# A spectral filter and a gated feed-forward block on one core: remainder blocks placed by small DMAs, first weights in pieces, one normalizing operation, the down projection in halves

## The chip, the cores and the metric

The kernel runs on one core of one Trainium2 chip. The metric is the device time of one execution in microseconds (us); lower is better. A core has five engines that each work through a list of instructions in order: TensorE (PE in the profile; its weight loads are a row of their own, PEld), VectorE (DVE), ScalarE (ACT), GpSimd (POOL) and SyncE (SP). SP issues most DMAs, POOL the others. Engines wait for one another on semaphores.

## The reference

The input x is [1, 2048, 576] in bf16. Two residual blocks follow each other:

```
def _A_ref(x, w_r, w_i):                     # spectral filter
    X = rfft2(x.astype(float32), axes=(-2, -1))
    X = X * (w_r + 1j * w_i)                 # w_r, w_i: [2048, 289]
    return irfft2(X, s=(2048, 576), axes=(-2, -1)).astype(bfloat16)

def _B_ref(x, w_gate, w_up, w_down):         # 576 -> 4608 -> 576
    return (gelu(x @ w_gate) * (x @ w_up)) @ w_down

h  = x + _A_ref(layernorm(x), w_r, w_i)
h2 = h + _B_ref(layernorm(h), w_gate, w_up, w_down)
```

The layer norms have no weights; gelu is the tanh form.

## The kernel before

The 2048 rows lie as 16 tiles of 128 rows in XO (tile c, 576 columns). The program is written as one list of operations; a helper, `Prog`, records for each what it reads and writes and puts in the semaphore waits. The order on every engine is the order in which operations are recorded, so a wait at the head of an engine's list holds up everything behind it. Three orders are written out by hand as strings of tokens.

**First stage (`SEQ1`, up to about 20 us).** The first layer norm's statistics, and the first step of the transform over rows, into U. SP loads x, tables and the filter weights (WS) meanwhile.

**Transform stage (`SEQF`, about 20 to 46 us).** For each of 16 groups i the list has: D (a matmul over columns; lower case d is its second half with the evacuation into CUS), B (matmul, evacuation into YS), T (two DVE multiplies of YS with the filter weights WS: the main 256 columns into TP, line 673, and the remaining 32 into TR), V (matmul, v its second half with the evacuation into V, line 607) and, for every four groups, R (matmul of the collected remainders TR). `VENG`, `DENG` and `BENG` say whether ACT or DVE evacuates. R's result goes through ACT into RB (line 703), and `st_R` then places it in VR by DVE multiplies with a mask of ones and zeros, MK (line 711): a block of 32 partitions of VR must hold its own group's numbers and zeros elsewhere. Before `SEQF` starts, POOL copies parts of WS to the other half of the partitions by DMA (`dup_w`). Behind the last of these, SP loads the tables DT and IT and the identity IDT (lines 747 to 749); `wg_load(0, 0)` at line 750 then loads the first quarter of the gate weights (POOL) and of the up weights (SP), each as one transfer of 512 rows and one of 64. `wg_load(1, 1)` and `wg_load(2, 2)` follow after `SEQF`.

**Inverse stage (`SEQ`, about 46 to 58.5 us).** For tiles 0 to 7: I (matmul of V and, in the second half i, of VR with DT, lines 802 to 809), E (its evacuation into GS; A, D and S name the engines: ACT, DVE, split), N and o (matmul with IT), a (add into XO on DVE, line 831). For tiles 0 to 3 also: s (sum of squares), q and c (square root and reciprocal), n (`norm`, lines 854 to 860: two operations, 576 columns and then the last 64 columns once more, so that HN has 640), u and U (transposes on TensorE with IDT), e (evacuation into HT0), and at last G0 and G1, the first gate/up products in two parts of 256 rows.

**Feed-forward part (from about 58.5 us).** Four blocks of 512 rows. In each, `gu_part` (line 917) computes gate and up for 36 column blocks f of 128, as 64-row matmuls of 512 columns that run in pairs on the two halves of the array; ACT applies gelu (line 925) and DVE multiplies (line 926) into AT. In the first block the inverse stage of tiles 8 to 15 is mixed in (`def_i`, `def_n`). Then `down` (lines 997 to 1009) multiplies AT by WD for four tiles of 128 rows: per tile two column halves of 288, each 36 matmuls with all 128 rows of the array (line 1004), then the residual add (line 1007) and the store. The last tile splits 448 and 128. The tiles of the next block are normalized and transposed by DMA while TensorE works.

Of the kernel before, what the change touches and what calls it, by code (L numbers as in the profile page):

```python
# [15 lines left out]
NT = 16  # L16
# [11 lines left out]
SEQF = """D1 D0 d1 D2 d0 d2 B1 D4 B0 d4 D3 T1 B2 T0 d3 D5 V1 d5 T2 v1 D6 B3 d6 B4 V0 B5 T3 v0 D7 T4 D8 d7 B6 d8 V3 R0 T5 v3 T6 r0 V2 B7 v2 D9 V5 d9 D10 v5 d10 V4 B9 T7 D12 v4 d12 B8 D11 T9 B10 d11 R1 D13 T8 T10 r1 d13 D14 B11 V6 d14 V7 v6 v7 T11 B12 V8 D15 v8 B13 T12 d15 B14 T13 V9 v9 T14 R2 r2 B15 V10 V12 v10 V13 v12 R3 T15 r3 V11 v13 V14 v11 v14 V15 R4 v15 r4""".split()  # L28
VENG = [('act',), ('dve',), ('act',), ('act',), ('act', 'dve'), ('act', 'dve'), ('act', 'dve'), ('act', 'dve'), ('act',), ('act',), ('act',), ('act',), ('act',), ('act',), ('act', 'dve'), ('act', 'dve')]
DENG, BENG = ['act', 'act', 'dve', 'act', 'act', 'act', 'dve', 'act', 'dve', 'act', 'act', 'act', 'dve', 'act', 'act', 'dve'], ['act', 'act', 'act', 'act', 'act', 'act', 'act', 'act', 'act', 'act', 'act', 'act', 'act', 'act', 'act', 'act']  # L30
QR = ((0, 1), (1, 2), (2, 3), (3, 4), (4, 8), (8, 16))
DEF0, DSTEP = 3, 4
SEQ = """I3 I1 i3 I2 E3S i1 i2 E1S N3 I0 o3 i0 a3 N1 E2A N2 E0S o1 I7 a1 s3A o2 N0 i7 o0 q3 s1A a2 c3 I5 a0 E7A s2D I6 q1 i5 E5A c1 s0D i6 E6A N7 I4 o7 n3P i4 q2 a7 n1P u3 q0 N5 U3 E4A c0 o5 e3A c2 u1 n2P U1 e1A N6 n0D u0 o6 U0 N4 a5 u2 e0A a6 U2 o4 G0 e2D a4 G1""".split()
# [296 lines left out]
def _build(nc, A_x, A_w_r, A_w_i, B_w_gate, B_w_up, B_w_down, out):  # L330
# [20 lines left out]
    VR = sb.alloc("VR", [128, NT, NG, 2, 4], BF16)  # L351
# [21 lines left out]
    MK = sb.alloc("MK", [128, 2, 8], BF16)  # L373
# [37 lines left out]
    RB = sb.alloc("RB", [128, 2, 2, NT, 2, 4], BF16)  # L411
# [217 lines left out]
    def wg_load(j, slot):  # L629
        f0, f1 = 1152 * j, 1152 * j + 1152  # L630
        tile = wg_tile(slot)
        for o, (eng, src) in enumerate(((POOL, B_w_gate), (SP, B_w_up))):
            P.dma(eng, tile[:, 4 * o:4 * o + 4, :], src[0:512, f0:f1].rearrange("(t p) f -> p t f", p=128), f"wgu{o}{j}{slot}", w=[("WG", slot, o)])
            P.dma(eng, tile[64 * o:64 * o + 64, 8, :], src[512:576, f0:f1], f"wgu{o}{j}{slot}", w=[("WG", slot, 2 + o)])
# [57 lines left out]
    def st_R(q, second):  # L692
        js = [i for i in range(4 * q, 4 * q + 4) if i < LAST] if q < 4 else [LAST]
        g0, n, b0 = GORD[js[0]], len(js), FB["R", q]

        def mm(h, o, t_, first, last, after):
            return P.op(PE, lambda t: t.matmul(bank(b0 + o, 0, 128, 0, 128), TR[64 * h:64 * h + 64, q % 2, o, t_, :], VT[64 * h:64 * h + 64, 1 + o if q == 4 else 0, t_, :], start=first, stop=last),
                        r=[("TR", q % 2, j) for j in range(4)] + ["VT"], w=[("PS", b0 + o)], after=after)

        halves(("R", q), second, [[0, 1]] * 2, mm)  # L700
        if not second:
            return
        ev(ACT, RB[:, q % 2, :, :, :, :].rearrange("p t n o e -> p o (t n) e"), banks(b0, 2, 128).rearrange("p o (a e) -> p o a e", e=4),
           [("PS", b0), ("PS", b0 + 1)], [("RB", q % 2)])
        for u in range((n + 1) // 2):
            m = min(2, n - 2 * u)
            for t_ in range(2):
                dst = VR[64 * t_:64 * t_ + 64, :, g0 + 2 * u:g0 + 2 * u + m, :, :].rearrange("p n g o e -> p n g (o e)")
                src = RB[64 * u:64 * u + 64, q % 2, t_, :, :, :].rearrange("p n o e -> p n (o e)").unsqueeze(2).to_broadcast([64, NT, m, 8])
                msk = MK[64 * u:64 * u + 64, 0:m, :].unsqueeze(1).to_broadcast([64, NT, m, 8])  # L710
                P.op(DVE, lambda v, dst=dst, src=src, msk=msk: v.tensor_tensor(dst, src, msk, op=ALU.mult),  # L711
                     r=[("RB", q % 2), "MK"], w=[("V", GORD[i], 2 + t_) for i in js[2 * u:2 * u + m]])
# [33 lines left out]
    P.op(SP, None, after=[last])  # L746
    P.dma(SP, DT[:, :, :].rearrange("p a b -> p (a b)"), dram["DTAB"][:, :], "dt", w=["DT"])
    P.dma(SP, IT[:, :, :, :].rearrange("p a b c -> p (a b c)"), dram["ITAB"][:, :], "it", w=["IT"])
    P.dma(SP, IDT[:, :], dram["EYE"][:, :], "eye", w=["IDT"])
    wg_load(0, 0)  # L750
    P.dma(SP, DP[:, :, :].rearrange("p a b -> p (a b)"), dram["DPAR"][:, :], "dp", w=["DP"])
    P.dma(SP, ITD[:, :, :].rearrange("p a b -> p (a b)"), dram["IDEF"][:, :], "itd", w=["ITD"])

    for w in SEQF:
        i = int(w[1:].rstrip("abc"))
        if w[0] in "Dd":
            st_D(i, w[0] == "d", DENG[i])
        elif w[0] == "B":
            st_B(i, BENG[i])
        elif w[0] == "T":  # L760
            if w[-1] in "ab":
                st_T(i, (0,) if w[-1] == "a" else (1,))
            else:
                st_T(i)
        elif w[0] in "Vv":
            st_V(i, w[0] == "v", VENG[i])
        elif w[0] in "Rr":
            st_R(i, w[0] == "r")


    P.alias(sum(wkeys, []) + sum(dup, []), [("WG", j, k) for j in (1, 2) for k in range(4)])
    for j in range(1, 3):
        wg_load(j, j)
# [3 lines left out]
    vtail = [("V", g, c) for g in range(NG) for c in range(2, 4)]  # L777
# [24 lines left out]
    def i_mm(c, second):  # L802
        b, e = SLOT["I", c], ends.setdefault(("I", c), [None, None])
        for j in range(2 + second):
            for r in range(2):
                o, r0 = r ^ (not second), 64 * r
                lhs = V[r0:r0 + 64, j, o, c, :, :, :] if j < 2 else VR[r0:r0 + 64, c, :, :, :]
                e[o] = P.op(PE, lambda t, r0=r0, o=o, j=j, lhs=lhs: t.matmul(bank(b + o, 0, 128, 0, KW), lhs, DT[r0:r0 + 64, 2 * o + j if j < 2 else 4, 0:KW], start=(not second and j == 0), stop=(second and j == 2)),  # L808
                            r=vk[j] + ["DT"], w=[("PS", b + o)], after=[e[o]] if second and j == 0 else [])
# [44 lines left out]
    def norm(c, eng=DVE):  # L854
        hs = c % 4
        q = lq(c)
        for i, (o0, o1, x0, x1) in enumerate(((0, D, 0, D), (D, 640, 512, D))):
            P.op(eng, lambda v, c=c, hs=hs, o0=o0, o1=o1, x0=x0, x1=x1: v.tensor_scalar(HN[:, hs, o0:o1], XO[:, c, x0:x1], NM[:, c:c + 1],
                                                                                        RS2[:, c:c + 1], op0=ALU.add, op1=ALU.mult),
                 r=[("X", c), ("NM", c), ("RS2", q)], w=[("HN", hs, i)])  # L860

    def turn_dma(c):
# [3 lines left out]
        for k in range(5):  # L866
            P.dma(SP, HT[:, k, 128 * (c % 4):128 * (c % 4) + 128], HN[:, hs, 128 * k:128 * k + 128], f"tr{c}",
                  r=[("HN", hs, 0), ("HN", hs, 1)], w=[("HT", q % 2, c % 4, k)], transpose=True)

    def turn_mm(c, second):  # L870
        hs, b0, e = c % 4, SLOT["u", c], ends.setdefault(("u", c), [None, None])
        plan = ((3, 0), (4, 1)) if second else ((0, 2), (1, 3), (2, 4))
        for j, ks in enumerate(plan):
            for r, k in enumerate(ks):
# [3 lines left out]
                            r=[("HN", hs, 0), ("HN", hs, 1), "IDT"], w=[("PS", b0 + o)], after=[e[o]] if second and j == 0 else [])  # L878
# [25 lines left out]
    def gu_part(m, second, c0=0, c1=512):  # L904
# [5 lines left out]
        for j in range(n):  # L910
            for half in range(2):
                o, wt = seqs[half][j]
                kt = 4 if wt == 8 else wt % 4
# [36 lines left out]
    fdead = ["DT", "IT", "J0", "J1", "ZD"] + [(n_, c) for n_ in ("ATB", "ATS") for c in range(NT)] + [("G", i // 2, i % 2) for i in range(10)] + [*[("Y", a) for a in range(NY)], ("RB", 0), ("RB", 1)]  # L950
# [4 lines left out]
    def def_i(c, second):  # L955
        e = ends.setdefault(("X", c), [None, None])
        for j in range(3):
            for r in range(2):
                o, r0 = r ^ (not second), 64 * r
                t_ = j if j < 2 else r  # L960
                lhs, rhs = (V[r0:r0 + 64, o, t_, c, :, :, :], DP[r0:r0 + 64, 2 * o + t_, :]) if j < 2 else (VR[r0:r0 + 64, c, :, :, :], DP[r0:r0 + 64, 4 + o, :])
# [35 lines left out]
    def down(tb, p):  # L997
        c = 4 * tb + p

        cut = 448 if c == NT - 1 else 288  # L1000
        for h, (d0, d1) in enumerate(((0, cut), (cut, D))):
            b = 2 * (p % 2) + h
            for k, f in enumerate([*range(36)] if tb == 0 else [*range(9, 36), *range(9)]):
                P.op(PE, lambda t, b=b, d0=d0, d1=d1, f=f, p=p: t.matmul(bank(b, 0, 128, 0, d1 - d0), AT[:, f, 128 * p:128 * p + 128],  # L1004
                                                                        WD[:, f, d0:d1], start=(f == 9 * (tb > 0)), stop=(f == (8 if tb else 35))),
                     r=[("AT", f), ("WD", f // 4)], w=[("PS", b)])
            P.op(DVE, lambda v, b=b, d0=d0, d1=d1, p=p, c=c: v.tensor_tensor(OS[:, p % 2, d0:d1], bank(b, 0, 128, 0, d1 - d0), XO[:, c, d0:d1], op=ALU.add),  # L1007
                 r=[("PS", b), ("X", c)], w=[("OS", p % 2, k) for k in (range(2) if d1 == cut and cut > 288 else (h,))])
            P.dma(SP, ov[:, c, d0:d1], OS[:, p % 2, d0:d1], f"so{p % 2}{h}", r=[("OS", p % 2, h)], w=[("OUT", p % 2, h)])
# [3 lines left out]
    for tb in range(4):  # L1013
# [26 lines left out]
        for p in range(4):  # L1040
            down(tb, p)
# [37 lines left out]
```

## Time and profile before

| what | value |
|---|---|
| median of 3 runs | 490.61 us (489.57 to 491.44) |
| profiled execution | 489.82 us, span 487.8 us |
| granted TensorE clock | 1.000 of full speed |
| PE busy in the span | 479.1 us, 98% |
| DVE / ACT / POOL busy | 188.6 / 147.2 / 43.2 us |
| masked multiplies, DVE (line 711) | 18, 0.22 to 0.29 us each |
| matmuls of down (line 1004), 288 columns | 1080 recorded, 286 ns each |
| norm on DVE (line 858) | 425 ns for 576 columns and 295 ns for 64 |
| norm on POOL (line 858) | 923 ns for 576 columns and 560 ns for 64 |
| output store | 1.6 us from issue to landing |

The span is the time from the first to the last instruction of the profiled execution; its time is 2.0 us longer. Matmuls are pipelined: a matmul's own duration (286 ns) is longer than the distance to the next one's start, so the distance is what counts. In a timeline line the first number is the start, the second the time from the first start to the last end of the xN instructions that were merged. For DMAs the row of the queue (SPq) is the time of issuing, not of moving the data.

### The profile page before, as it was taken

Reading aid. Unit: us, or ns where it says so; the run is one execution under the profiler, and the core shown is the slowest. Engines: PE = TensorE matmul, PEld = TensorE weight load, DVE = VectorE, ACT = ScalarE, POOL = GpSimd, SP = SyncE. Lnnn points to the kernel's source line nnn. Section 1 sums busy time; section 2 is a strip of 40 time slices with the busy share of each in tenths; the row PEclk is TensorE's granted clock in tenths of the full one; section 3 lists DMA queues with packets and bytes.
Section 4 is the critical chain, followed back from the end, with each engine's and each line's share of the span. In section 5 each row is a group of like instructions: output and inputs, shape, how many; then the busy total and the mean of one; then the engine's idle time right before and its main releaser. Section 6 shows DMA issues by size and latency. Waiting matters only on the chain.

```text
span 487.8 us, 10721 instructions
## 1 busy us (share of the span) xinstructions
PE 479.1 (98%) x4791; PEld 286.9 (59%) x4792; DVE 188.6 (39%) x389; ACT 147.2 (30%) x294; POOL 43.2 (9%) x77
## 2 busy tenths in 40 slices
PE   7998999999999999999999999999999999999998
PEld 3876675555577744444577644444677444444775
DVE  7898746666511134333311144333211233333011
ACT  6997754343400022233200022332100123323000
POOL 5852631000300000000000000000000000000000
PEclk9999999999999999999999999999999999999999
DMA  8969998211350000100000001000000000000000
GB/s 283 231 160 321 353 329 270 74 26 26 110 170 20 16 18 19 23 1 1 1 19 19 13 20 23 15 1 2 6 19 19 7 1 1 1 0 1 13 19 18
DMA packets 25533, 32.65 MB, mean 67 GB/s; under 512 B 11664, under 2 KB 18096, under 8 KB 25488
## 3 DMA queue, kind: packets, MB, share of 16 engines
q1 hardware_dynamic: 22048, 18.27, 13.0%
q0 software_dynamic: 3440, 13.70, 8.8%
q8 instruction: 37, 0.61, 0.5%
q14 instruction: 8, 0.07, 0.1%
HBM read 26.01 MB, written 2.36 MB: 58 GB/s over the span
## 4 chain that ended last, share of the span: by engine, by line
PE 91%; DVE 3%; DMA 2%; POOL 2%; ACT 1%; issue 1%; DVEq 0%; POOLq 0%
PE PS L917 57%; PE PS L1004 29%; PE PS L537 1%; DMA WS<-WS 1%; DVE TP L673 1%; DVE XO L831 1%; DMA WS<-in_A_w_r_dram 1%; ACT U L563 1%; PE PS L962 1%; POOL WS L725 1%; POOL WS L240 1%; PE PS L808 0%; DVE VR L711 0%; PE PS L979 0%; PE PS L825 0%
## 5 line engine op out<-in xcount | busy, mean ns | idle before, releaser
L917 PE MATMUL PS<-HT,WG 64*128 64x512 bf16 (+1 forms) x2142 | 233.5, 372 | 0.0
L917 PEld LDWEIGHTS PS<-HT,WG 64*128 64x128 bf16 x2142 | 109.8, 94 | 111.0 <-issue 0.9
L925 ACT ACTIVATE GL<-PS 128x512 bf16<-128x512 f32 x144 | 85.7, 596 | 282.4 <-PE PS L917 274.4
L926 DVE TENSOR_TENSOR AT<-GL,PS 128x512 bf16<-128x512 bf16 x144 | 98.8, 687 | 165.1 <-ACT GL L925 165.1
L1004 PE MATMUL PS<-WD,AT 128*128 128x288 bf16 (+2 forms) x1152 | 141.8, 286 | 0.0
L1004 PEld LDWEIGHTS PS<-WD,AT 128*128 128x128 bf16 x1152 | 111.0, 98 | 31.5 <-ACT GL L925 1.3
L1007 DVE TENSOR_TENSOR OS<-PS,XO 128x288 bf16<-128x288 f32 (+2 forms) x32 | 14.6, 458 | 123.3 <-PE PS L1004 123.3
L917 PE MATMUL PS<-HT,WGX 64*128 64x512 bf16 x486 | 53.4, 376 | 0.0
L917 PEld LDWEIGHTS PS<-HT,WGX 64*128 64x128 bf16 x486 | 23.7, 94 | 28.8
L640 PE MATMUL PS<-FT,U 64*128 64x288 bf16 x160 | 14.1, 284 | 0.3 <-DVE V L607 0.2
L834 ACT ACTIVATE OS<-XO,NM 128x576 bf16<-128x576 bf16 x14 | 10.8, 774 | 11.4 <-DVE XO L983 11.4
L681 PE MATMUL PS<-VT,TP 64*128 64x128 bf16 x256 | 11.2, 217 | 0.1
L673 DVE TENSOR_TENSOR TP<-YS,WS 128x1024 bf16<-128x1024 bf16 x16 | 11.0, 689 | 0.4 <-ACT YS L607 0.2
L240 POOL DMA_DIRECT2D WD<-in_B_w_down_dram x9 | 6.8, 759 | 49.1 <-PE PS L979 49.1
L563 ACT ACTIVATE U<-PS 128x384 bf16<-128x384 f32 (+2 forms) x31 | 10.5, 427 | 1.4 <-PE PS L552 1.3
L495 DVE BATCH_NORM_STATS2 ST<-XO 128x6 f32<-128x288 bf16 x26 | 10.0, 441 | 1.9 <-DMA XO<-in_A_x_dram 1.7
L607 ACT ACTIVATE YS<-PS 128x576 bf16<-128x576 f32 x16 | 10.1, 661 | 0.3 <-PE PS L660 0.2
L552 PE MATMUL PS<-ATS,XO 128*128 128x128 bf16 x96 | 8.1, 219 | 1.9 <-POOL ATS L521 1.7
L681 PEld LDWEIGHTS PS<-VT,TP 64*128 64x128 bf16 x256 | 8.4, 94 | 2.1 <-PE PS L681 0.2
L537 PE MATMUL PS<-ZD 128*128 128x512 bf16 x19 | 7.5, 560 | 1.5 <-POOL ZD L430 1.5
L552 PEld LDWEIGHTS PS<-ATS,XO 128*128 128x128 bf16 x96 | 6.9, 98 | 3.1 <-POOL ATS L521 2.5
L640 PEld LDWEIGHTS PS<-FT,U 64*128 64x128 bf16 x160 | 7.0, 94 | 2.7 <-DVE V L607 0.7
(83 smaller groups left out, 213.5 us busy)
## 6 DMA issues: line engine op xcount, KB each, us to landing
WD<-in_B_w_down_dram POOLq DMA_DIRECT2D x9, 576.0 KB, 13.1
WG<-in_B_w_gate_dram POOLq DMA_DIRECT2D x4, 1152.0 KB, 9.8
WG<-in_B_w_up_dram SPq DMA_DIRECT2D x4, 1152.0 KB, 9.4
out_dram<-OS SPq DMA_DIRECT2D x30, 72.0 KB, 1.6
XO<-in_A_x_dram SPq DMA_DIRECT2D x3, 576.0 KB, 7.2
WGX<-in_B_w_up_dram SPq DMA_DIRECT2D x1, 1152.0 KB, 5.6
WGX<-in_B_w_gate_dram POOLq DMA_DIRECT2D x1, 1152.0 KB, 9.9
HT<-HN SPq DMA_TRANSPOSE x60, 2.4
```

The lines of the kernel that those rows point to most:

```text
L240: fn = lambda e: e.dma_start(out_ap, in_ap)
L537: P.op(PE, lambda t: t.matmul(bank(b), ZD[:, 0:128], ZD[:, :], start=True, stop=True), r=["ZD"], w=[("PS", b)])
L552: P.op(PE, lambda t, b=b, lhs=lhs, p0=p0, p1=p1, s=s, e=e, o=o, c=c: t.matmul(bank(b, p0, p1, o, o + 128), lhs, ATS[:, c, :], start=s, sto ...
L563: fn = (lambda v: v.tensor_copy(dst, src)) if eng == DVE else (lambda a: a.activation(dst, src, ACTF.Copy))
L640: return P.op(PE, lambda t: t.matmul(bank(b0 + o, 0, 128, 0, 2 * HK), U[64 * h:64 * h + 64, us, 2 * i:2 * i + 2, :, :], FT[64 * h:64 * h + ...
L673: P.op(DVE, lambda v, dst=dst, y4=y4, w4=w4: v.tensor_tensor(dst, y4, w4, op=ALU.mult), r=[("Y", sl), *dup[(i >= 5) + (i >= 8) + (i >= 12) ...
L681: return P.op(PE, lambda t: t.matmul(bank(b0 + o, 0, 128, 128 * c, 128 * c + 128), TP[64 * h:64 * h + 64, z, o, t_, c:256:2], VT[64 * h:64 ...
L917: op = P.op(PE, lambda t, h0=h0, kt=kt, wt=wt, b=b, s=(not second and j == 0), e=(second and j == n - 1): t.matmul(bank(b, 0, 128, c0, c1) ...
L925: P.op(ACT, lambda a: a.activation(GL[:, s2, :], bank(b0), ACTF.Gelu_apprx_tanh), r=[("PS", b0)], w=[("GL", s2)])
L926: P.op(DVE, lambda v: v.tensor_tensor(AT[:, f, :], GL[:, s2, :], bank(b0 + 1), op=ALU.mult), r=[("GL", s2), ("PS", b0 + 1)], w=[("AT", f)])
L1004: P.op(PE, lambda t, b=b, d0=d0, d1=d1, f=f, p=p: t.matmul(bank(b, 0, 128, 0, d1 - d0), AT[:, f, 128 * p:128 * p + 128], WD[:, f, d0:d1], ...
L1007: P.op(DVE, lambda v, b=b, d0=d0, d1=d1, p=p, c=c: v.tensor_tensor(OS[:, p % 2, d0:d1], bank(b, 0, 128, 0, d1 - d0), XO[:, c, d0:d1], op=A ...
```

## The change

Four edits, with the hand-written orders and engine choices redone around them:

1. **Remainder blocks.** VR gets another layout ([128, 16 groups, 2, 4, 16 tiles] instead of tiles first) and is set to zero by POOL at the start; MK and the masked multiplies are gone. For R0 to R2, RB is evacuated as before (R0 by DVE, R1 and R2 by ACT) and eight DMAs per R on SP, of 32 partitions with 256 bytes each, put the blocks where they belong. For R3 and R4 ACT and DVE evacuate straight from PSUM into VR, a block of 32 partitions at a time. The permutation moves into R's matmul, whose right operand is read with a step.
2. **First weights.** The first quarter of gate and up is loaded by SP in ten pieces; each piece waits until TensorE has done everything recorded before a token of the order (`LOADS`). The tables DT, IT and IDT are issued behind r1, DP and ITD behind i6. Slots 1 and 2 and WD are issued after the first gate/up product, G0.
3. **One normalizing operation.** The 640 columns of HN are written by one operation that reads XO as two overlapping runs of 320 columns; the weight tiles' order follows that.
4. **Down in halves.** All tiles but the last use 64-row matmuls in pairs, in two passes per tile; the halves change places in the second pass, and the passes of different tiles are interleaved ("0 1 0 2 1 3 2 3").

```
+SEQF = """D1 D0 d1 D2 d0 d2 B1 D3 B0 T1 T0 d3 D4 B2 d4 D5 V1 T2 d5 v1 D7 B4 d7 B3 D6 B5 d6 V2 T4 V0 T3 v2 v0 D8 B7 T5 d8 D10 B6 d10 D9 T6 B8 d9 D11 R0 T7 d11 V5 r0 V3 v5 v3 V4 B9 v4 D13 B10 d13 T8 V6 D12 v6 T9 d12 V7 T10 V9 v7 R1 v9 r1 B11 B13 T11 D14 B12 T12 d14 D15 V8 d15 v8 B14 T13 T14 R2 r2 B15 V10 V11 v10 V13 v11 V12 v13 T15 v12 V14 V15 v14 v15 R3 R4 r3 r4""".split()
+VENG = [('act', 'dve'), ('dve',), ('act', 'dve'), ('act',), ('act',), ('act', 'dve'), ('act',), ('act', 'dve'), ('dve',), ('act', 'dve'), ('act',), ('act',), ('act', 'dve'), ('act',), ('act', 'dve'), ('act', 'dve')]
+DENG, BENG = [... 'dve' at 2 and 7, else 'act'], [... 'dve' at 6, 9 and 11, else 'act']
+LOADS = {"r1": "t", "v8": "0", "v10": "1", "v11": "2", "v13": "3", "v12": "4", ".i0": "5", ".i1": "6", ".N3": "7", ".i4": "8 9", ".i6": "d"}
+RENG = ['dve', 'act', 'act', 'act', 'act']
+SEQ = """I2 I3 i2 E2A I0 i3 i0 N2 I1 o2 E3A i1 E0S a2 N0 N3 o0 I4 o3 E1S s2A q2 a0 N1 i4 s0A E4A a3 o1 c2 q0 I6 I5 n2P a1 i6 i5 s3D E6A I7 c0 N4 E5A i7 s1D n0P o4 a4 u2 N6 U2 E7A o6 q1 q3 c1 u0 N5 U0 c3 o5 n3P e2A n1D e0A u1 U1 N7 e1A a6 u3 a5 o7 a7 U3 e3D G0 G1""".split()
...
-    P.op(POOL, lambda g: g.memset(MK[:, :, :], 0.0), w=["MK"])
...
+    P.op(POOL, lambda g: g.memset(VR[:, :, :, :, :], 0.0), ...)
...
     # st_R
-        ev(ACT, RB[:, q % 2, ...], banks(b0, 2, 128)..., [("RB", q % 2)])
-        ... P.op(DVE, lambda v, dst=dst, src=src, msk=msk: v.tensor_tensor(dst, src, msk, op=ALU.mult), ...)
+        if q < 3:
+            ev(RENG[q], RB[:, q, :, :, :, :].rearrange("p t o e n -> p o t (e n)"), banks(b0, 2, 128).rearrange("p o (t x) -> p o t x", t=2), keys, [("RB", q)])
+            for j, i in enumerate(js):
+                for t_ in range(2):
+                    P.dma(SP, VR[64 * t_ + 32 * (j % 2):64 * t_ + 32 * (j % 2) + 32, GORD[i], :, :, :], RB[32 * j:32 * j + 32, q, t_, :, :, :], f"r{q}", ...)
+            return
+        for j, i in enumerate(js):
+            for e, o0, o1 in (((ACT, DVE)[j], 0, 2),) if q == 3 and j < 2 else ((ACT, 0, 1), (DVE, 1, 2)):
+                for t_ in range(2):
+                    ... ev(e, dst, src, keys[o0:o1], [("V", GORD[i], 2 + t_, o0)])
...
+    def hold(eng=SP):
+        P.op(eng, None, after=[P.ops[PE][-1]])
+    def tab_load():
+        P.op(SP, None, after=[last])
+        ... DT, IT, IDT
+    def tab2_load():
+        hold()
+        ... DP, ITD
+    def wg0_part(k):
+        hold()
+        src = (B_w_gate, B_w_up)[k % 2]
+        if k < 8:
+            P.dma(SP, WG3[:, 0, 4 * (k % 2) + k // 2, :], src[(0, 128, 320, 448)[k // 2]:(128, 256, 448, 576)[k // 2], 0:1152], "wg00")
+        else:
+            P.dma(SP, WG3[64 * (k % 2):64 * (k % 2) + 64, 0, 8, :], src[256:320, 0:1152], "wg00", ...)
...
     # norm
+        x2 = bass.AP(x.tensor, x.offset, [list(x.ap[0]), [256, 2], [1, 320]])
+        P.op(eng, lambda v: v.tensor_scalar(HN[:, hs, :].rearrange("p (a b) -> p a b", a=2), x2, NM[:, c:c + 1], RS2[:, c:c + 1], op0=ALU.add, op1=ALU.mult), ...)
...
     for w in SEQ:
         ...
+        loads("." + w)
+        if w == "G0":
+            hold(SP), hold(POOL)
+    for j in range(1, 3):
+        wg_load(j, j)
...
+    def down_pass(tb, p, second):
+        fs, b0 = forder(tb), 2 * ((3, 0, 1, 2)[p] if tb == 0 else p)
+        e = ends.setdefault(("Z", tb, p), [None, None])
+        for j, f in enumerate(fs):
+            for r in range(2):
+                h, r0 = r ^ second, 64 * r
+                e[h] = P.op(PE, ... matmul(bank(b0 + h, 0, 128, 0, 288), AT[r0:r0 + 64, f, 128 * p:128 * p + 128], WD[r0:r0 + 64, f, 288 * h:288 * h + 288], ...)
+        if second:
+            for h in range(2):
+                down_out(tb, p, h, 288 * h, 288 * h + 288, b0 + h, False)
...
+        for w in "0 1 0 2 1 3 2 3".split() if tb < 3 else "0 1 0 2 1 2".split():
+            first = ("Z", tb, int(w)) not in ends
+            down_pass(tb, int(w), not first)
+    down_last(3, 3)
```

More of the change, by code (lines that the diff above doesn't have):

```diff
@@ L912, in gu_part @@
                 o, wt = seqs[half][j]
-                kt = 4 if wt == 8 else wt % 4
+                kt = 2 if wt == 8 else (0, 1, 3, 4)[wt % 4]
                 h0 = 64 * half
@@ L995, in deferred, with down_out @@
             fn(c, second)
-    def down(tb, p):
+    def down_out(tb, p, h, d0, d1, b, both):
         c = 4 * tb + p
-        cut = 448 if c == NT - 1 else 288
+        P.op(DVE, lambda v: v.tensor_tensor(OS[:, p % 2, d0:d1], bank(b, 0, 128, 0, d1 - d0), XO[:, c, d0:d1], op=ALU.add),
+             r=[("PS", b), ("X", c)], w=[("OS", p % 2, k) for k in (range(2) if both else (h,))])
+        P.dma(SP, ov[:, c, d0:d1], OS[:, p % 2, d0:d1], f"so{p % 2}{h}", r=[("OS", p % 2, h)], w=[("OUT", p % 2, h)])
@@ new lines, in forder @@
+    def forder(tb):
+        return [*range(36)] if tb == 0 else [*range(9, 36), *range(9)]
+    def down_pass(tb, p, second):
[4 more added lines that the diff above has]
+                h, r0 = r ^ second, 64 * r
+                e[h] = P.op(PE, lambda t, f=f, h=h, r0=r0, j=j: t.matmul(bank(b0 + h, 0, 128, 0, 288), AT[r0:r0 + 64, f, 128 * p:128 * p + 128], WD[r0:r0 + 64, f, 288 * h:288 * h + 288],
+                                                                         start=(not second and j == 0), stop=(second and j == 35)),
+                            r=[("AT", f), ("WD", f // 4)], w=[("PS", b0 + h)], after=[e[h]] if second and j == 0 else [])
+        if second:
+            for h in range(2):
+                down_out(tb, p, h, 288 * h, 288 * h + 288, b0 + h, False)
@@ L1001, in down, with down_last @@
+    def down_last(tb, p):
+        cut = 448
         for h, (d0, d1) in enumerate(((0, cut), (cut, D))):
[L1002 to L1005, printed above, removed]
+            b = 2 * p + h
+            for j, f in enumerate(forder(tb)):
+                P.op(PE, lambda t, b=b, d0=d0, d1=d1, f=f, j=j: t.matmul(bank(b, 0, 128, 0, d1 - d0), AT[:, f, 128 * p:128 * p + 128], WD[:, f, d0:d1], start=(j == 0), stop=(j == 35)),
@@ L1006, in down @@
                      r=[("AT", f), ("WD", f // 4)], w=[("PS", b)])
-            P.op(DVE, lambda v, b=b, d0=d0, d1=d1, p=p, c=c: v.tensor_tensor(OS[:, p % 2, d0:d1], bank(b, 0, 128, 0, d1 - d0), XO[:, c, d0:d1], op=ALU.add),
-                 r=[("PS", b), ("X", c)], w=[("OS", p % 2, k) for k in (range(2) if d1 == cut and cut > 288 else (h,))])
-            P.dma(SP, ov[:, c, d0:d1], OS[:, p % 2, d0:d1], f"so{p % 2}{h}", r=[("OS", p % 2, h)], w=[("OUT", p % 2, h)])
+            down_out(tb, p, h, d0, d1, b, h == 0)
```

76 lines of the change are left out of this document (33 added, 43 removed).

## The prediction

> **What bounds the kernel now.** I read the page first, then the chain of waits, then busy time by stage, then the timelines of the queues that the change touches.
>
> ```profile
> span 487.8 us, 10721 instructions
> PE 479.1 (98%) x4791; PEld 286.9 (59%) x4792; DVE 188.6 (39%) x389; ACT 147.2 (30%) x294; POOL 43.2 (9%) x77
> ```
>
> ```profile
> 28.93 5.47 DMA WS<-WS
> ...
> 45.36 0.75 DVE V L607 x2
> 46.10 0.14 issue
> 46.24 1.89 PE PS L808 x28
> 48.13 0.54 issue
> ...
> 58.61 6.25 PE PS L917 x92
> ...
> 133.79 35.39 PE PS L1004 x288
> 169.17 70.04 PE PS L917 x648
> ```
>
> From 58.6 us on, the chain is TensorE alone: gate/up (L917) and down (L1004), four times over, to 485.5. No wait there is worth removing; only the cost of a matmul and of the switch between the two forms counts. Whatever else the change can win lies ahead of 58.6.
>
> ```profile
> 20.98:34.44 13.46, 13.45 (x268) 10.09 (x264) 12.68 (x29) 12.85 (x26) 9.52 (x18) 1.00 0.66 161
> 34.44:46.57 12.13, 10.75 (x254) 8.14 (x250) 11.85 (x35) 10.68 (x24) 1.92 (x3) 1.00 1.01 318
> 46.57:58.55 11.98, 10.49 (x183) 6.95 (x179) 8.91 (x22) 8.90 (x20) 6.18 (x10) 1.00 1.03 340
> ```
>
> The columns after the window are its length, then busy PE, weight loads, DVE, ACT, POOL. In the middle stage DVE is busy 11.85 of 12.13 us: it bounds it. The stage starts at 34.4, when the second copy of WS has landed (first fence). In the last stage before the feed-forward part no engine is full.
>
> **The change part by part.** All terms are against the profiled execution (span 487.8, its time 489.82; the median of the three runs shown is 490.61, 0.79 above it).
>
> *Down in halves.* Each 128-row matmul of 288 columns becomes two of 64 rows on the two halves of the array. Cadence: 288 of the old in 35.39 us is 0.1229 each; ten 64-row ones of the same width (23.66, last fence) are five pairs: (0.78 - 0.284) / 4 = 0.124, within reading error. So one pair costs what one matmul did: 15 tiles x 72 pairs stay as they were, and each ns by which I am wrong costs 1.08 us. What goes is the switch of form:
>
> ```profile
> 132.96 0.83 PE L917 MATMUL PS<-HT,WG 64*128 64x512 bf16 x6
> 133.72 0.42 PE L1004 MATMUL PS<-WD,AT 128*128 128x288 bf16 x2
> ```
>
> ```profile
> 168.52 0.65 PE L1004 MATMUL PS<-WD,AT 128*128 128x288 bf16 x4
> 169.11 0.39 PE L917 MATMUL PS<-HT,WG 64*128 64x512 bf16 x2
> ```
>
> The last gate/up matmul starts at 132.96 + 0.83 - 0.376 = 133.41, down 0.31 later instead of 0.216; the way back is 169.11 - (168.52 + 0.65 - 0.286) = 0.22 instead of 0.123. That is 0.095 each. There are seven; the last tile keeps the old form, so one comes back: 6 x 0.095 = 0.6 us won. The semaphore that a tile's second pass waits for belongs to a pass with another tile's 4.4 us pass behind it: no cost.
>
> *Masked multiplies go.* DVE loses 18 of them: 14 x 0.29 + 4 x 0.22 = 4.9 us. It gains evacuations moved by the new order (three YS at 0.67, V shares, one RB, six small tail pieces at about 0.2) and loses three CUS. From T8 on I count 8 x 0.74 (T), 0.67 (B11), 0.66 (v8), 5 x 0.35 (V halves), 6 x 0.2 (tail): 10.2 us from 34.44, so 44.7, with some stalls 45.2, against 46.57 before. T8 would be ready by 33.5, but waits for the copy that lands at 34.40, because what releases it upstream is untouched. ACT comes out equal (27.5 against 27.8 us summed).
>
> *The small DMAs.* R0, R1 and R2 issue eight each on SP, 24 in all, and SP takes its list in order: R0, R1, then DT, IT and the identity (placed behind r1 now, at 37.50 before), weight piece 0, then R2. Behind R2 wait pieces 1 to 9 and the second tables. The waits for TensorE themselves hold nothing up before R2: v8's matmuls are done near 40, SP gets there after 42. The first I matmul that reads VR waits for R2's last landing. So the spacing s of SP's issues is the crux. Rows:
>
> ```profile
> 2.60 0.43 SPq L240 DMA_DIRECT2D ATB<-c_atab  x1
> 3.07 0.91 SPq L240 DMA_DIRECT2D XO<-in_A_x_dram  x2
> ...
> 23.06 1.23 SPq L240 DMA_DIRECT2D WS<-in_A_w_r_dram  x2
> ```
>
> Plain two-dimensional loads at the start follow each other at 0.47; strided 32-row ones at 23 us at 0.64; a lone one takes 0.33 (DT, the output stores), so 0.37 with the gap. The new ones are plain, with few rows: I take 0.47 and keep 0.37 and 0.64 as ends. R1's evacuation by ACT stands behind V9, which waits for T9: 34.44 + 1.48, matmuls and evacuation, some 37.0. From there: 8 x 0.47 = 40.8; three tables 1.5, 42.3; piece 0, 42.8; R2, 46.55; landing as the stores do, 1.6: 48.15. This is later than DVE's 45.2 and decides. Before, the same point (VR read, 46.98 in the timeline) stood at about 47.0. At 0.37 it is 46.2; at 0.64 R0 itself runs to 38.0 and the point is 52.6. (R0 starts near 32.9: from 22.1, where the copies of WS end, DVE has 8.6 us of work ahead of T7 in the new list, 0.8 of stalls, T7 and the RB evacuation.) For any spacing that the trace shows, SP ends after DVE: the multiplies' 4.9 us are not what is won.
>
> R's right operand is now read with a step of 4 elements, VR's weights with 16. TP's weights with a step of 2 load in 94 ns like contiguous ones, so I take nothing; if such a load took twice that, 24 pairs would be 0.07 us longer, 1.6 us.
>
> *From there to the first gate/up.* Before, POOL's norms made it late:
>
> ```profile
> 52.45 1.69 POOL L858 TENSOR_SCALAR HN<-XO,NM,RS 128x576 bf16<-128x576 bf16 x2 [5.15 <-DVE RS L844]
> 54.31 1.75 POOL L858 TENSOR_SCALAR HN<-XO,NM,RS 128x576 bf16<-128x576 bf16 x2 [0.17 <-POOL HN L858]
> 56.23 1.32 POOL L858 TENSOR_SCALAR HN<-XO,NM,RS 128x576 bf16<-128x576 bf16 x2 [0.17 <-DVE HN L858]
> ```
>
> Three pairs, 5.1 us, then 1.0 to the first gate/up at 58.55. One operation of 640 columns costs 0.92 x 640/576 = 1.03, so the row shrinks to 3.3, and DVE's own chain takes over: a2 starts 2.2 after the VR point (rest of I2, its evacuation, N2 and o2), then 5.8 us of DVE work to the last reciprocal, 1.15 for POOL's last norm, 0.55 for u3, o7, U3: 9.7, with stalls 10.2 (9.7 to 11.3). Before, 46.98 to 58.55 took 11.6. So gate/up starts at 48.15 + 10.2 = 58.35, 0.2 earlier. DVE's norms inside the feed-forward part get shorter under TensorE's cover: nothing.
>
> *Weight pieces.* Before, the gate half was issued at 31.83 and shared the DMA engines with the tables (DT took 5.1 us to land). Now pieces 8 and 9 leave when i4 is done, 4.3 after the VR point; two issues and a landing of some 3 us end at about 8.3, under 10.2. Cover is 1.9 us. Slots 1 and 2 and WD start at 58 instead of 44; slot 1 is read 20 us later and took 15 at most. POOL's fill of VR: from ZD's 0.53 for 512 columns, 2048 cost 1.8, ending at 3.45 against the first x at 3.70, hidden.
>
> **Sum.** -0.6 (switches) - 0.2 (start of gate/up) = -0.8: 489.0 for the profiled execution; on the footing of the median 489.8.
>
> **The rivals.**
>
> *SP is quick* (0.25). At 0.37 the VR point is 46.2 and gate/up starts at 56.4: -2.2 - 0.6 = -2.8, 487.8; with the shorter 9.7, or with DVE's 45.2 as the limit, down to 486.3. For it: the lone issues at 0.33. Against: no train in the trace is so dense.
>
> *SP is slow* (0.20), the one that ends slower. At 0.64 the VR point is 52.6 and gate/up starts at 62.8: +4.25 - 0.6 = +3.7, 494.3. For it: SP's W loads keep that spacing, whatever their size. Against: they are strided, and issued while x and W fill the DMA engines. It decides over the bound from s = 0.60 on (point at 51.3, +2.4).
>
> *Issue rate of TensorE* (0.04). Down now starts a matmul and a weight load every 61 ns, for 35 us at a stretch. If pairs settled at 124 ns instead of 122.6, it would cost 1080 x 1.4 = 1.5 us: 491.3. Against: the V stage starts 64-row matmuls of 128 columns in pairs 56 to 60 ns apart.
>
> ```profile
> 41.69 0.82 PE L681 MATMUL PS<-VT,TP 64*128 64x128 bf16 x22
> ...
> 23.66 0.78 PE L640 MATMUL PS<-FT,U 64*128 64x288 bf16 x10
> ```
>
> The Trainium skill (TensorE: Matmul & The Clock Gate, "Wait — 56ns, not 53.3ns?") says that without hardware decode about 62 ns go into each matmul, a bound once the array's work is shorter; a pair would be 124 ns. Here 22 matmuls start within 0.82 - 0.217 us, 29 ns each, so the trace does not bear that bound out.
>
> *The change does not reach the path* (0.03): the last weight piece lands later than 10.2 after the VR point, as late loads did here (10.6 us for the gate rest). It would then add what it is late, 1 to 4 us, 491 to 493.5.
>
> **How the numbers follow.** The forecast has 0.48. A measurement of this kernel can tell about 0.5%, 2.45 us, from no change. The quick case is faster by more than that in most of its chance, and the forecast's own short side adds a little: faster 0.27. Slow SP beyond 0.60 and late weights: slower 0.19. The rest, 0.54, lies within. The range takes the quick case at 9.7 on its low side and the slow one up to s = 0.62 on its high side: 486.6 to 493.6. The forecast's own range, s from 0.42 to 0.56, is 488.7 to 491.9.
>
> **What would show it.** Right: SP's small DMAs 0.45 to 0.5 apart; TensorE waiting at its first VR matmul near 48 while DVE and ACT idle; gate/up first at about 58.3; 36 pairs of down in 4.41 us; no gap over 0.13 at the switch; norms on POOL near 1.03. Wrong: the VR matmul released by DVE or ACT (SP quick), or after 51 (SP slow); pairs over 123 ns; a first gate/up that waits for WG.

## The result and the profile after

The changed kernel takes 496.49 us (median of 4 runs, 495.86 to 497.51), the kernel before 490.86 beside it (4 runs, 489.57 to 491.44): ratio 1.012, 95% interval 1.0092 to 1.0148. It is slower, and 2.9 us above the upper end of the range predicted. The profiled execution took 496.92 us. From its page:

```profile
span 495.1 us, 12880 instructions
...
PE 479.8 (97%) x5872; PEld 282.4 (57%) x5872; DVE 182.9 (37%) x367; ACT 147.6 (30%) x296; POOL 44.9 (9%) x72
...
PEclk9999699999999999999999999999999999999999
```

TensorE's busy time is nearly what it was (479.8 for 479.1); the span grew by 7.3 us. One slice of 12.4 us, the fifth, was not granted the full clock. The chain of waits shows what stands there:

```profile
42.18 1.59 SPq L243
...
51.48 1.76 DMA VR<-RB
53.38 2.38 PE PS L829 x18
...
62.63 1.43 POOL HN L880
66.52 6.20 PE PS L938 x92
```

Where the chain before ran from DVE's last evacuations straight into the I matmuls at 46.24, it now goes through SP's queue, through a landing in VR, and reaches gate/up (L938) at 66.5 instead of 58.6. Busy time by stage (length; busy PE, weight loads, DVE, ACT, POOL; granted clock; DMA share; GB/s):

```profile
34.44:46.57 12.13, 9.85 (x244) 7.90 (x238) 10.88 (x29) 10.71 (x26) 0.00 (x0) 1.00 0.12 22
46.57:53.38 6.81, 1.05 (x13) 0.46 (x14) 0.00 (x0) 0.00 (x0) 0.00 (x0) 0.67 0.53 180
53.38:59.15 5.77, 5.77 (x49) 4.16 (x51) 1.60 (x3) 2.88 (x6) 0.00 (x0) 0.50 0.83 260
59.15:66.42 7.27, 6.91 (x127) 4.89 (x124) 6.60 (x15) 6.11 (x14) 3.34 (x3) 1.00 0.62 187
```

DVE did lose the multiplies (it is busy 10.88 us for 11.85, as it took over evacuations) and is done before 46. Then for 6.8 us no engine but TensorE has anything to do, and TensorE itself works for only 1.05 of them; for the next 5.8 us it works at clock 0.50. What the idle stretch waits for is in the timelines of SP's queue and of TensorE:

```profile
32.72 12.32 SPq L243 DMA_DIRECT2D VR<-RB  x16
45.08 0.58 SPq L243 DMA_DIRECT2D DT<-c_dtab  x1
45.70 0.43 SPq L243 DMA_DIRECT2D IT<-c_itab  x1
46.17 0.43 SPq L243 DMA_DIRECT2D IDT<-c_eye  x1
46.65 0.43 SPq L243 DMA_DIRECT2D WG<-in_B_w_gate_dram  x1
47.12 4.95 SPq L243 DMA_DIRECT2D VR<-RB  x8
```

```profile
48.27 1.04 PE L829 MATMUL PS<-DT,V 64*128 64x288 bf16 x12 [3.60 <-DMA DT<-c_dtab]
53.38 0.46 PE L829 MATMUL PS<-DT,VR 64*128 64x288 bf16 x2 [4.07 <-DMA VR<-RB]
```

The sixteen small DMAs of R0 and R1 occupy SP without a pause from 32.72 to 45.04. DT stands behind them and lands at 48.2: TensorE waits 3.6 us. R2's eight end at 52.07 and the last lands at 53.24: it waits 4.1 us more. The clock was halved from 48.91 to 59.15.

The tail went as forecast. The switch of form (last gate/up matmul at 140.25 + 1.46 - 0.376 = 141.33, down at 141.54) is 0.21 instead of 0.31:

```profile
140.25 1.46 PE L938 MATMUL PS<-HT,WG 64*128 64x512 bf16 x12
141.54 1.14 PE L1038 MATMUL PS<-WD,AT 64*128 64x288 bf16 x16
```

Four points are used below for every run, all from the matmuls of the profiled execution: the VR point (first matmul that reads VR), G0 (first gate/up matmul), X (from one to the other) and the tail (from G0 to the last matmul). All are taken from start to start.

| kernel | VR point | X | G0 | tail | clock at one half |
|---|---|---|---|---|---|
| before | 46.98 | 11.57 | 58.55 | 426.68 | none |
| after | 53.38 | 13.04 | 66.42 | 426.09 | 48.91 to 59.15 |

### The profile page after: what moved, and what is told of

It reads as the page before. It is cut to its first block, busy times and chain, and to the rows that moved or that the text cites. A ratio compares the mean times of both kernels' runs of the same rounds, so it can differ in the third digit from the quotient of the medians.

```text
span 495.1 us, 12880 instructions
## 1 busy us (share of the span) xinstructions
PE 479.8 (97%) x5872; PEld 282.4 (57%) x5872; DVE 182.9 (37%) x367; ACT 147.6 (30%) x296; POOL 44.9 (9%) x72
## 4 chain that ended last, share of the span: by engine, by line
PE 88%; DMA 3%; SPq 3%; POOL 2%; DVE 2%; issue 1%; ACT 0%; POOLq 0%; DVEq 0%
PE PS L938 57%; PE PS L1038 27%; SPq L243 3%; PE PS L1050 2%; DMA XO<-in_A_x_dram 1%; DMA WS<-WS 1%; PE PS L846 1%; PE PS L829 1%; DVE ST L495 1%; DMA WS<-in_A_w_r_dram 1%; PE PS L988 1%; POOL WS L729 1%; POOL WS L243 1%; DVE XO L852 0%; PE PS L1005 0%
## 5 line engine op out<-in xcount | busy, mean ns | idle before, releaser
L938 PE MATMUL PS<-HT,WG 64*128 64x512 bf16 (+1 forms) x2142 | 233.3, 372 | 0.0
L938 PEld LDWEIGHTS PS<-HT,WG 64*128 64x128 bf16 x2142 | 106.0, 94 | 114.1 <-DVE AT L947 0.2
L1038 PE MATMUL PS<-WD,AT 64*128 64x288 bf16 x2160 | 132.9, 283 | 0.0
L1038 PEld LDWEIGHTS PS<-WD,AT 64*128 64x128 bf16 x2160 | 103.3, 94 | 29.8
L1025 DVE TENSOR_TENSOR OS<-PS,XO 128x288 bf16<-128x288 f32 (+2 forms) x32 | 13.3, 453 | 125.5 <-PE PS L1038 118.0
L938 PE MATMUL PS<-HT,WGX 64*128 64x512 bf16 x486 | 53.4, 376 | 0.0
L938 PEld LDWEIGHTS PS<-HT,WGX 64*128 64x128 bf16 x486 | 23.2, 94 | 29.2
L829 PE MATMUL PS<-DT,V 64*128 64x288 bf16 x64 | 7.4, 338 | 3.6 <-DMA DT<-c_dtab 3.6
L682 PE MATMUL PS<-VT,TP 64*128 64x128 bf16 x256 | 9.6, 217 | 0.3 <-DVE TP L674 0.3
L243 POOL DMA_DIRECT2D WG<-in_B_w_gate_dram x9 | 6.1, 678 | 34.2 <-DMA WG<-in_B_w_gate_dram 30.6
L1050 PE MATMUL PS<-WD,AT 128*128 128x448 bf16 (+1 forms) x72 | 9.0, 286 | 0.0
L607 ACT ACTIVATE CUS<-PS 128x576 bf16<-128x576 f32 x14 | 8.9, 654 | 0.2 <-PE PS L641 0.2
```

The costliest lines, as they stand in the source:

```text
L243: fn = lambda e: e.dma_start(out_ap, in_ap)
L938: op = P.op(PE, lambda t, h0=h0, kt=kt, wt=wt, b=b, s=(not second and j == 0), e=(second and j == n - 1): t.matmul(bank(b, 0, 128, c0, c1) ...
L1025: P.op(DVE, lambda v: v.tensor_tensor(OS[:, p % 2, d0:d1], bank(b, 0, 128, 0, d1 - d0), XO[:, c, d0:d1], op=ALU.add), r=[("PS", b), ("X", ...
L1038: e[h] = P.op(PE, lambda t, f=f, h=h, r0=r0, j=j: t.matmul(bank(b0 + h, 0, 128, 0, 288), AT[r0:r0 + 64, f, 128 * p:128 * p + 128], WD[r0:r ...
L1050: P.op(PE, lambda t, b=b, d0=d0, d1=d1, f=f, j=j: t.matmul(bank(b, 0, 128, 0, d1 - d0), AT[:, f, 128 * p:128 * p + 128], WD[:, f, d0:d1], ...
```

## The experiments

Theory: SP's train of small DMAs, with the table queued in it, makes TensorE wait, and the wait costs the clock. Rivals: the new order of the transform stage, the normalizing operation, the halves, or the late weights. Medians stand beside the kernel before on the same chip (490.3 to 491.0).

**Half of the small DMAs on GpSimd.**

```
-P.dma(SP, VR[64 * t_ + ...], RB[...], f"r{q}", ...)
+P.dma((SP, POOL)[t_], VR[64 * t_ + ...], RB[...], f"r{q}{t_}", ...)
```

> The changed kernel with half of the small DMAs (one of each pair) issued by POOL, which has nothing to do from 31.8 to 61 us, and the other half by SP; all else as changed. Theory A (SP's train of issues at 0.63 us sets the first VR matmul, at 53.4): R1's four on SP run from 37.9 to 40.4, the tables and piece 0 to 42.4, R2's four to 44.9, the last lands near 46.8. First VR matmul at 46.5 to 48, full clock throughout, first gate/up at 57 to 58.5, time 487 to 490. Theory B (the new orders themselves make the inverse stage longer, about 13 us from the VR matmul to gate/up): VR matmul at 47 too, but gate/up only at 60, time 490.5 or more.

Measured: 492.24 us, ratio 1.0036 (1.0021 to 1.0051). VR point 49.40, G0 62.43, tail 426.08. SP has twelve issues fewer, R1's part of its train ends at 40.8 instead of 45.0, and everything behind it comes 4 us earlier; nearly three quarters of the loss are gone. But X is still 13.04: TensorE stood idle for 1.13 and 2.17 us, and the clock was halved from 48.35 to 55.17. The forecast for the VR point (46.5 to 48) was missed: R2's last DMA is issued at 45.41 and lands at 49.16.

**Dummy matmuls in the wait.** Matmuls of zeros (15 before I2, 18 before its second half) keep TensorE busy.

```
+    def warm(n, b):
+        for _ in range(n):
+            P.op(PE, lambda t: t.matmul(bank(b), ZD[:, 0:128], ZD[:, :], start=True, stop=True), ...)
...
+        if w in ("I2", "i2"):
+            warm(*((15, ...) if w == "I2" else (18, 7)))
```

> The changed kernel with 15 and 18 matmuls on zeros of 128 x 512 put ahead of I2 and i2, so that TensorE does not stand idle while it waits for DT and for VR. The DMAs are untouched, so the first VR matmul stays at 53.4. Theory A1 (the half clock from 48.8 to 59.1 us is a second loss on top of SP's train): full clock, gate/up 1.5 to 2.8 us earlier than 66.4, time 493.7 to 495. Theory B (half clock costs nothing since DVE and ACT set the pace, the order is what is slow): 496 to 497.

```profile
46.87 3.18 PE L960 MATMUL PS<-ZD 128*128 128x512 bf16 x14 [0.16 <-issue]
50.31 0.66 PE L829 MATMUL PS<-DT,V 64*128 64x288 bf16 x8 [0.26 <-DMA DT<-c_dtab]
50.91 4.06 PE L960 MATMUL PS<-ZD 128*128 128x512 bf16 x18
```

Measured: 495.92 us, ratio 1.011 (1.0083 to 1.0137), so the time hardly moved. The trace says why: X fell to 10.29, as it should at full clock, but the VR point stood at 56.09, because in this execution an earlier stretch at half clock (13.2 to 16.6) had moved the whole front back by about 2.4 us (SP's train starts at 35.17 for 32.72). The run shows the price of the half clock behind the wait (13.04 - 10.29 = 2.75 us). The one execution of the four that had the full clock throughout took 494.45, within the 493.7 to 495 expected; by the median the remedy stays inconclusive.

**The masked multiplies back, all else as changed.** VR's layout, MK and the multiplies come from the kernel before, the orders stay new.

> The changed kernel with the first edit alone taken back: VR in its old layout, mask and 18 DVE multiplies, no small DMAs; the new orders, weight pieces, norm and halves stay. Theory A: without the train SP issues the tables at 38 or so, the first VR matmul comes at 46.5 to 48 (DVE is the limit again), gate/up at 57 to 58.5, time 487 to 490. Theory B (orders or weight pieces at fault): gate/up after 59, time 491 or more.

Measured: 490.30 us, ratio 0.9999 (0.9979 to 1.0019). VR point 49.18, X 10.23, tail 426.04, full clock. Undoing the first part alone takes the loss away. It gives no gain: what X and the tail win, the VR point loses. TensorE idles 1.21 us at 39.04 and 1.15 us at 44.67, and its first VR matmul waits for DVE's last multiply. That the new order was not made for these multiplies is the likely reason; the next run bears it out.

**The multiplies back, and the old order of the transform stage.** As the last, with `SEQF` and the engine choices of before.

> The changed kernel with its first part undone (remainder blocks placed by masked multiplies on VectorE) and with the order and the engines of the first stage's work taken from the kernel before; pieces of the first weights, new second order, one normalizing operation and halves stay. Theory (all that is lost lies in part one with its order; the rest is worth about 1.3 us ahead of gate/up and 0.6 behind): first remainder matmul at 46.5 to 47.5 us, 10.3 us to the first gate/up matmul at 57 to 57.8, 426.05 from there on, median 488.3 to 489.3, faster than before by 0.3 to 0.5%. Rival (pieces released by TensorE's progress hold the table or the weights up where the old order runs): first gate/up matmul at 58.5 or later, median 490 or more.

Measured: 488.16 us, ratio 0.9955 (0.9939 to 0.997). VR point 47.50, X 10.24, G0 57.73, tail 426.04. So the other three parts with the new `SEQ` are worth 1.3 us in X and 0.6 in the tail, and the whole loss lies in the first part.

**Parts three and four on the kernel before.**

> The kernel before with the third and the fourth edit alone (one normalizing operation, down in halves). The step of the prediction on halves says 0.6 us less from the first gate/up to the end; the step on norms says that POOL's three norms shrink from 5.1 to 3.3 us and gate/up starts 0.8 to 1.5 earlier than 58.55: time 488.5 to 489.5. Rival (POOL's norms were hidden): gate/up stays at 58.5, time about 490.2.

Measured: 498.89 us, ratio 1.0168 (1.0136 to 1.0199), a miss: VR point 46.78, but X 19.66.

```profile
59.77 1.25 POOL L240 DMA_DIRECT2D WG<-in_B_w_gate_dram  x2 [8.11 <-DMA WG<-in_B_w_gate_dram]
61.07 0.87 POOL L860 TENSOR_SCALAR HN<-XO,NM,RS 128x640 bf16<-128x640 bf16 x1
```

The operation itself is quick (0.87 us). What makes it late is the line above it. The new load of a weight block is two transfers under one key, so the second waits until the first has landed, and GpSimd's list stands still for 8.1 us with the norms behind it. In the changed kernel these loads come after G0, where nothing waits for GpSimd. With keys of their own:

```
-                P.dma(eng, ..., w=[("WG", slot, o)])
+                P.dma(eng, ..., w=[("WG", slot, o + 4 * u)])
```

The operations that read the weights wait for the new keys too.

> The kernel before with one normalizing operation and the down projection in halves, and with the two halves of each 512-row weight load under keys of their own, so that the second does not wait for the first. Theory (these two parts cost nothing by themselves, and the late GpSimd in the run without own keys was that wait): first remainder matmul at 46.8 us, first gate/up matmul at 57 to 58.3, 426.0 us from there to the last matmul, median 488.5 to 490. Rival (one operation of 576 elements as 2 x 320 is itself slow on GpSimd, or halves of loads crowd the queue): first gate/up matmul after 60 us, median over 492.

Measured: 489.26 us, ratio 0.9978 (0.9966 to 0.999). VR point 46.92, X 10.98, tail 426.40 (a late WD transfer holds TensorE's weight loads for 0.49 us at 137). GpSimd's lines L860 start at 52.33, 53.99 and 55.58 and take 0.87, 1.42 and 1.06.

**Down in halves alone on the kernel before.**

> The kernel before with the down projection in halves and nothing else. Theory (a pair of 64-row matmuls costs what one 128-row matmul did, and only the switches of form go): 426.0 to 426.1 us from the first gate/up matmul to the last matmul in place of 426.68, the first gate/up matmul at 58.5 as before, ratio 0.998 to 0.9995. Rival (the pairs settle at 124 ns because TensorE has to start a matmul and a weight load every 61 ns): 427.5 to 427.7 us, ratio 1.001 to 1.003.

Measured: 490.24 us, ratio 0.9991 (0.9977 to 1.0005). The total can't tell 0.6 us from nothing, but the trace can: tail 426.03 against 426.68.

**Tables early, all DMAs on SP.** The table's wait for the last duplicated weight is taken out, and it is issued before the first operation of the transform stage.

```
-LOADS = {"r1": "t", "v8": "0", ...}
+LOADS = {"v8": "0", ...}
     def tab_load():
-        P.op(SP, None, after=[last])
...
+    tab_load()
     for w in SEQF:
```

> The changed kernel with one edit: the three tables of the first stage are issued before the encoder, without the wait for the last duplicated weight; all 24 small DMAs stay on SP. Theory (train and table are two separate losses, and the train alone still sets the first remainder matmul): first table matmul at 44.5 to 45.5 us, the third group of small DMAs is issued from 45.5 on at 0.63 us each and lands at 52, first remainder matmul at 51.5 to 52.5, a wait of 3 to 4.5 us ahead of it, so that the half clock comes again and 12 to 13 us lie between it and the first gate/up matmul; median 494 to 496. Rival (the late table was the cause): first remainder matmul at 47 to 49, full clock, median 488 to 490.

```profile
45.72 0.43 PE L829 MATMUL PS<-DT,V 64*128 64x288 bf16 x4
47.28 0.67 PE L829 MATMUL PS<-DT,V 64*128 64x288 bf16 x8 [1.13 <-DVE VR L607]
51.70 0.46 PE L829 MATMUL PS<-DT,VR 64*128 64x288 bf16 x2 [3.76 <-DMA VR<-RB]
```

Measured: 494.82 us, ratio 1.0097 (1.0061 to 1.0132). The wait for DT is gone, the wait for VR is not. The train alone still sets the VR point, 1.7 us earlier without the tables in it. Half clock 51.19 to 54.61, X 11.63.

**Tables early and half of the small DMAs on GpSimd.** Weight piece 0 also moves behind R2, by `LOADS`.

> The changed kernel with every second small DMA issued by GpSimd, and the three tables of the first stage issued before the encoder starts, without the wait for the last duplicated weight; the first piece of the first weights after r2. Theory (the loss is SP's train of DMAs, the table queued in it, and the half clock that the idle TensorE brings): first table matmul right behind the last tail matmul at about 44.7 us, first remainder matmul at 46.5 to 48.5, no stretch at clock 0.5, 10.3 us from there to the first gate/up matmul, which starts at 56.8 to 58.8; median 488 to 490. Rival (what is left after the DMAs were shared out is the new order, not the table): first remainder matmul at 49.4 as with shared DMAs alone, with a wait of over 3 us ahead of it and half clock behind it; median 492.

```profile
34.73 11.69 SPq L243 DMA_DIRECT2D VR<-RB  x12
46.46 0.58 SPq L243 DMA_DIRECT2D WG<-in_B_w_gate_dram  x1
```

Measured: 488.07 us, ratio 0.9951 (0.9934 to 0.9969). SP's line now has pauses between groups. VR point 48.53, X 10.34 at full clock, G0 58.87, though this execution had lost time to a stretch at half clock at 14.1 to 17.5. The remainder blocks by DMA cost nothing any more once they are off a single queue. That they pay by themselves is not shown: this version and the one with masks in the old order both beat both kernels, by about the same (488.07 and 488.16). By the executions with the full clock throughout they are 487.09 to 487.32 (three of six) and 487.28 to 488.44 (five of six).

**What sets the issue time?** The same 24 DMAs in three other forms. None of them places the remainder blocks; the times alone count.

```
wide_form:   VR[:, g, t_] <- RB[:, q, t_, 0]             128 partitions x 128 bytes, from SBUF
dram_narrow: VR[32 rows, g] <- EYE[32 rows, :]           32 partitions x 256 bytes, from DRAM
dram_wide:   VR[:, g, t_] <- EYE[:, 64 t_:64 t_ + 64]    128 partitions x 128 bytes, from DRAM
```

> The changed kernel, but each of the 24 small DMAs moves 128 partitions x 128 bytes in place of 32 partitions x 256 bytes (twice the bytes, to and from other addresses, so the remainder blocks are not placed and the output's values mean nothing; everything waits as before). Theory A (the issue on SP costs by the form: few partitions are slow): they go 0.47 us apart, the table of the first stage is issued about 41 instead of 45.1 us, TensorE's first remainder matmul starts at 48.5 to 50 us instead of 53.4, the median is 492 to 494. Theory B (0.63 us is what SP needs at that time whatever the form): 0.6 us or more apart, first remainder matmul at 53 to 54 us, median 496 to 497.

> The changed kernel with the 24 small DMAs reading the same 32 partitions x 256 bytes from a constant table in DRAM in place of the evacuated buffer in SBUF (so the remainder blocks are not placed and the output's values mean nothing; waits and destinations as before). Theory C (a source in SBUF makes the issue slow): 0.43 busy, 0.47 apart. Theory D (anything but whole rows of 128 partitions is slow): 0.59 busy, 0.63 apart, first remainder matmul at about 53.4 us.

> As the run before, but 128 partitions x 128 bytes from the table in DRAM (again not the remainder blocks; output without meaning). Theory C (source in SBUF): 0.43 busy, 0.47 apart, first remainder matmul at 49 to 50.5 us. Theory E (128 bytes a partition, or a queue that is already full, is slow whatever the source): 0.60 busy, 0.64 apart, first remainder matmul at 53 to 54. If this one is fast and the 32-partition one slow, both the source's place and the number of partitions count.

The lines of SP's queue for the last group of eight, first `wide_form`:

```profile
47.17 4.97 SPq L243 DMA_DIRECT2D VR<-RB  x8
```

then `dram_narrow`:

```profile
45.10 3.68 SPq L243 DMA_DIRECT2D VR<-c_eye  x8
```

and `dram_wide`:

```profile
45.20 3.75 SPq L243 DMA_DIRECT2D VR<-c_eye  x8
```

A single one takes 0.60, 0.42 and 0.43 us, 0.04 more to the next; the times are 496.18 (median of four runs, ratio 1.0113, 1.0091 to 1.0135), 493.68 and 492.74 (one run each). For these copies, which all end in SBUF, the issue is slow with the source in SBUF, whether 32 or 128 partitions, and quick from the table in DRAM in both forms. Theory A falls; B's numbers came in `wide_form` (VR point 53.50), but the DRAM forms are quick at the same place in the list, so B falls too; C holds for these copies, D and E fall. A source in SBUF alone does not make an issue slow: the output stores, from SBUF to DRAM, take 0.33 us, and 0.43 right behind another. Why the copies inside SBUF are slow is not shown; the strided WS loads from DRAM at 0.64 say that they are not the only slow ones.

The two DRAM forms are also the prediction's own case, issues 0.47 apart. Their VR points are 50.96 and 50.47 instead of 48.15, and both have half clock behind them. So the spacing alone does not account for the miss.

## Why the prediction was wrong, point by point

**The time of SP's train, the step that failed.** The term that was mis-sized is the spacing s, 0.47 for a measured 0.63, and the odd long issue had no term at all. The VR point was to be 48.15 and stood at 53.38, 5.2 us later:

- *0.47 for s.* It was taken from plain loads out of DRAM; between 0.63 and 0.64 was true. R0 and R1 end SP's train at 45.04; the forecast had 40.8. Sixteen issues at 0.63 from 32.72 end at 42.9, so 2.1 us come from the spacing; R2's eight took 4.95 for the 3.75 that they took at 0.47 from DRAM, 1.2 more.
- *Two issues of 1.72 and 1.59 us* (at 35.35 and 42.18, the second in the chain above) make up the other 2.1 us. The sum had no term for them. The kernel before has such ones: its SP timeline at 38.96 shows two weight issues in 2.15 us, one of them of 1.58. `dram_narrow` has two as well, 1.69 in the train and 1.15 at a table.
- The landing took 1.3 us from the end of the last issue instead of 1.6: -0.3. (The stores' 1.6 counts from the start of an issue.)
- R1's evacuation ended at 37.85, not at 37.0. In the changed kernel this is hidden, as SP reaches R1's DMAs at 39.02. In `dram_wide`, where R0's train is shorter, it ended at 38.67, and SP waited for it: part of the 2.3 us by which that VR point came later than 48.15.

The rival "SP is slow" (0.20) named this mechanism, its place and its point of decision: 52.6 against 53.38. That the two are so close is partly luck: it also took the tables at 0.64, which went at 0.47, and had no term for the long issues; its 494.3 lacks the half clock. It got too low a chance because of two arguments. One was that the 0.64 of the WS loads came from DMA engines that were full. They were at 0.12 in this stage, and the spacing stayed. The other was that only strided transfers are slow. A nearer row stood in the trace of before, GpSimd's copies from WS to WS, the only plain copies there inside SBUF: six in 3.59 us, 0.60 each. It is a hint and no more, for GpSimd's loads of WS from DRAM took 0.58 and 0.60 as well.

```profile
28.27 3.59 POOL L240 DMA_DIRECT2D WS<-WS  x6 [2.10 <-issue]
```

**A missing term: the clock.** X was to be 10.2 and measured 13.04. At full clock it is 10.2 to 10.3: 10.23 (`masked`), 10.24 (`masked_oldorder`), 10.29 (`warm_clock`), 10.34 (`tables_first`), 10.27 in the middle. So the working of X was right, and the 2.8 us are the half clock, which no rival had:

| kernel | TensorE idle before the VR point, us | half clock behind the VR point | X above 10.27 |
|---|---|---|---|
| after | 3.60 and 4.07 | 5.77 us | 2.77 |
| split_issue | 1.13 and 2.17 | 5.77 | 2.77 |
| dram_narrow | 2.38 and 2.55 | 4.16 | 1.97 |
| dram_wide | 0.67, 0.29 and 2.94 | 3.22 | 1.51 |
| wide_form | 3.77 and 3.40 | 3.15 | 1.49 |
| tables_only | 1.13 and 3.76 | 2.91 | 1.36 |
| tables_first | 1.13 | none | 0.07 |

In each row with half clock the loss is 0.47 or 0.48 of the time at half clock. The Trainium skill (TensorE: Matmul & The Clock Gate, "What's actually happening") says that the gate halves the clock after an idle window of about 3.4 us and gives it back after a busy one of that length; its "Terms" puts the cost at the throttled time x one half. The traces agree on the length and the cost: the stretches here last 3.41, 6.83 and 10.24 us, and the share is 0.47. They do not bear out that a whole window has to be idle: in the 3.41 us ahead of the halving TensorE had stood idle for 1.70 us (`wide_form`) to 3.25 us (`tables_only`) in the rows above. It is not certain at 2 us either: near 11 us an idle time of 2.1 us brought a stretch of half clock in `warm_clock` and `tables_first`, and the same in `wide_form` and `dram_wide` brought none. A wait of 4 us ahead of dense work is thus priced at up to 7.

**Sum.** G0 came 8.1 us later than forecast (66.42 for 58.35): 5.2 from SP, 2.8 from the clock. That is the whole error of 7.9 us in the profiled execution (496.92 for 489.0).

**Down in halves: right.** -0.6 forecast, -0.59 measured in the change, -0.65 alone. Pairs start 122 ns apart, and a block of 288 takes 35.16 us from first to last start, as the 288 whole matmuls did before (35.17). The issue-rate rival (0.04) falls: matmuls at 61 ns held for 35 us at a stretch.

**Multiplies gone: right that it wins nothing, half the size.** DVE ends at 45.99, 0.6 us earlier than before and not 1.4 (45.2 forecast); the evacuations that it took over fill most of the room. Since SP ends later, this won nothing by itself.

**Norm on GpSimd: about right.** 0.87, 1.42 and 1.05 us for 1.03 each. **VR's fill:** 1.805 us for 1.8, hidden. **Weight pieces: right.** TensorE never waited for them, so the rival of late weights (0.03) falls.

**Weights read with a step of 16: mis-sized, off the path.** The loads take 141 to 142 ns on average at full clock (`tables_first`, lines 829 and 988) for 94, where I had put nothing; the matmuls beside them hide nearly all of it (X is 10.34 in `tables_first`, which has them, and 10.24 in `masked_oldorder`, which has not).

## What to carry to other kernels

Count DMA instructions on a queue as work on an engine: each has its issue time, even when the DMA engines are nearly idle, and what stands behind them pays for all of them. Take the issue time from a row with the same source and destination memory, and allow for the odd issue of over a microsecond. When a sum makes TensorE idle for some 2 us or more within 3.4 us, allow for half clock behind it and for about half of that time as loss, and ask first whether the table or the block that it waits for can leave on another queue or earlier.

## What the runs showed of the hardware

- An SP issue of a copy inside SBUF took 0.59 to 0.60 us with 32 or with 128 partitions, one into the same place from a table in DRAM 0.42 to 0.43, a store from SBUF to DRAM 0.33 alone and 0.43 right behind another. On GpSimd the small DMAs took 0.50.
- In each of these kernels two to four issues of SP between 17 and 49 us take 1.0 to 2.0 us, whatever they move. What they wait for stays open.
- The half clock came in one to three whole stretches of 3.41 us, and also after two idle times of 1.13 and 2.17 us (`split_issue`); it did not come after 1.21 and 1.15 us (`masked`).
- Weight loads of 64x128 from elements 16 apart took 141 to 142 ns on average at full clock, contiguous ones 94.
